# Two PSUM banks taken out of a shared tile after the attention stage, and a count loaded into registers earlier

## The chip, the cores and the metric

The kernel runs on one core of one Trainium2 chip. The metric is device time in microseconds (us) of that core; smaller is better. The engines are TensorE (PE, its weight loads apart as PEld), VectorE (DVE), ScalarE (ACT), GpSimd (POOL) and SyncE (SP, which issues most DMAs). An instruction that belongs to the engine's own sequencer (register loads, branches, semaphores, drains) carries a q behind the engine's name in the rows, as SPq.

## The reference, cut to what matters

Linear attention, then a mixture of eight experts of which each token uses two, then one large MLP. In code, with batch 4, 8 heads, 576 positions, head size 64 (so 2304 tokens of width 512):

```python
def phi(x):
    proj = einsum('bhsd,df->bhsf', x, w_phi)
    proj = proj - max(abs(proj), axis=-1)
    return concatenate([exp(proj), exp(-proj)])
q_p, k_p = phi(q), phi(k)
kv, z = einsum('bhsf,bhsd->bhfd', k_p, v), sum(k_p, axis=2)
x = (q_p @ kv) / (q_p . z + 1e-6)                  # -> [2304, 512]
logits = x @ w_gate + log1p(exp(x @ w_noise)) * noise
top2_w, top2 = softmax over the two largest of the 8 logits
x2 = sum over the two: top2_w * (relu(x @ w1[e]) @ w2[e])      # F = 1024
out = square(relu(x2 @ w_in)) @ w_out                          # 512 -> 2048 -> 512
```

## The kernel before

**Numbers.** All large products are float32 by three matmuls: each operand is split into a high and a low part (`hi_lo`, lines 94 to 96: ACT copies the high part, DVE subtracts), and high·high, low·high and high·low are added up in one PSUM bank. So every matmul of line 92 (`mm`) comes in threes, as `w31h,hh`, `w31l,hh`, `w31h,hl`.

**Order.** The program runs under a manual schedule: each engine executes its instructions in the order in which the code is written, and semaphores hold it where another engine's result is missing.

**Stages.** Attention, with the gating of the experts woven into it (some 0 to 263 us of the trace). At its end the tokens are ranked within their experts: `r_3b` (line 652, PE) counts, `r_4` (line 667, DVE) adds the counts to `runs`, the running number of tokens of each expert, `r_4b` makes `slots`, and `r_5` (line 737, POOL) scatters the rows of x to `xg_d` in device memory, at most CAP = 640 slots an expert. Then the experts, in ten parts `pt` (263 to 720 us; experts 0 and 7 are cut in two; 0 already starts inside the attention stage), and the last MLP in five blocks of up to 512 tokens (720 to 1124 us), called m.

**An expert part.** `x_t` (line 175) turns the gathered rows by PE transposes and splits them. Then for each of the eight column groups f: `e_1` (line 190) makes hidden activations in the banks M0 and M1, from which ACT makes `hh` (relu, line 213) and DVE `hl` (line 210); `e_2` (line 223) adds the second product, one group later, into five accumulators `YP[j]`, one for each 128 tokens, j = 0 to 4, which keep their bank over all f. After the last f, `e_y` (line 218) copies each accumulator out by ACT (`y`, line 220) and SP stores it. At a boundary between two experts the main loop (line 1104) issues the last group of the old expert for j = 0, 1, 2, then the first `e_1` of the new one, then j = 3, 4. The last MLP has the same form: `l_t` (line 981) turns the input x2 of a block, `l_1` (line 994) makes `h2h` and `h2l`, `l_2` (line 1013) adds into the same accumulators and copies them out as `o` (by ACT, line 1029, or DVE, line 1027).

**Banks.** PSUM has eight banks here: Tk, KV, M0, M1, N0, N1 as tiles of one bank, and one tile of two banks, `pair` (line 79), which holds the tags Tq and P. `bank` (line 81) hands out a tile or a half of `pair`. Dependences are kept by tile: a write to one half of `pair` waits for the last reader of either half. The attention stage needs the two banks as one tile for the q products and the norms; the accumulators use Tq as j = 0 and P as j = 2 (`ACC`, line 146).

**The end.** A token count above CAP would need a slow path. `runs` is reduced to its largest value and cast by DVE, then loaded into a register of all five engines (`values_load`, line 1162), and `tc.If(most > CAP)` (line 1165) branches around the slow path, which is not taken here. Both stand behind all other work. Line 1255 is the end of the program, where the engines are drained and meet.

Of the kernel before, what the change touches and what calls it, by code (L numbers as in the profile page):

```python
# [9 lines left out]
FT = mybir.dt.float32  # L10
FR = mybir.dt.float32r
BF = mybir.dt.bfloat16
I32 = mybir.dt.int32
U16 = mybir.dt.uint16
AF = mybir.ActivationFunctionType
OP = mybir.AluOpType
AX = mybir.AxisListType
# [15 lines left out]
def kernel(  # L33
# [15 lines left out]
    nc = tc.nc  # L49
# [5 lines left out]
    NT = B * S  # L55
# [4 lines left out]
    DC = DM // 128  # L60
# [4 lines left out]
    consts = ctx.enter_context(tc.tile_pool(name="consts", bufs=1))  # L65
# [3 lines left out]
    psum = ctx.enter_context(tc.tile_pool(name="psum", bufs=1, space=bass.MemoryType.PSUM))  # L69
# [6 lines left out]
    x_d = dram.tile([NT, DM], FT, name="x_d")  # L76
    g_d = dram.tile([NT, E], FT, name="g_d")

    pair = psum.tile([128, 2, 512], FT, tag="pair", name="pair")

    def bank(tag, shape):
        if tag not in PAIR:
            return psum.tile(shape, FT, tag=tag, name=tag)
        names = "abc"[:len(shape) - 1]
        n = 1
        for x in shape[1:]:
            n *= x
        return pair[:, PAIR.index(tag), :n].rearrange(
            f"p ({' '.join(names)}) -> p {' '.join(names)}", **dict(zip(names, shape[1:])))
# [4 lines left out]
    def hi_lo(hi, lo, src):  # L94
        nc.scalar.activation(hi, src, AF.Copy)  # L95
        nc.vector.tensor_sub(lo, src, hi.bitcast(FT))  # L96
# [6 lines left out]
    runs = consts.tile([128, E], FT)  # L103
# [39 lines left out]

    NJ = CAP // 128
    NF = F // 128
    ACC = ["Tq", "KV", "P", "N0", "N1"]
    parts = [(0, 0, JA), (0, JA, NJ)] + [(e, 0, NJ) for e in range(1, E - 1)] + [(E - 1, 0, JA), (E - 1, JA, NJ)]
    XG, XT, HT, YP, xp = {}, {}, {}, {}, [None]

# [25 lines left out]
    def x_t(pt, j):  # L175
        e = parts[pt][0]
        if pt not in XT:
            n = RA if pt == 0 else CAP
            XT[pt] = (x_tile(pt, [128, DC, n], FR, "xth", ("kp", 2)), x_tile(pt, [128, DC, n], FR, "xtl", ("kp", 2)))
            if pt == NP - 2:  # L180
                XT[pt + 1] = XT[pt]
        t = bank(["Tk", "M0", "M1"][j % 3], [128, DC, 128])
        for d in range(DC):
            nc.tensor.transpose(t[:, d], XG[pt, j][:, d * 128:d * 128 + 128], ident)  # L184
        c = x_cols(pt, j)
        hi_lo(XT[pt][0][:, :, c], XT[pt][1][:, :, c], t)
# [36 lines left out]
    def e_2(pt, f, js=None):  # L223
# [4 lines left out]
        for j in range(j0, j1) if js is None else js:  # L228
            if f == 0:
                YP[j] = bank(ACC[j], [128, DM])  # L230
            c = slice((j - j0) * 128, (j - j0) * 128 + 128)
# [5 lines left out]

    with ExitStack() as actx:
        xp[0] = ap_ = actx.enter_context(tc.tile_pool(name="attn", bufs=1))

        KT, KTT, VT, VTT, QT, QTT, NZ = {}, {}, {}, {}, {}, {}, {}

# [545 lines left out]
        for n in range(NU + 2):  # L788
            b, i = divmod(n, 9)
# [96 lines left out]
        e_2(0, NF - 1)  # L886


    wpb[0] = ctx.enter_context(tc.tile_pool(name="wpb", bufs=1))

    with ExitStack() as ectx:
        xp[0] = ep = ectx.enter_context(tc.tile_pool(name="experts", bufs=1))
# [88 lines left out]
        def l_t(m, i):  # L981
            ya, _ = YA.pop((m, i))
            if i == 0:
                X2[m] = [ep.tile([128, DC, 512], FR, name="x2", tag=x, bufs=1)
                         for x in (("xth", "xtl") if m % 2 == 0 else ("xg", "wd"))]
            t = bank("Tk" if m else ("Tk", "Tq", "KV", "M0")[i], [128, DC, 128])
            for d in range(DC):
                nc.tensor.transpose(t[:, d], ya[:, d * 128:d * 128 + 128], ident)  # L988
            c = slice(i * 128, i * 128 + 128)
            hi_lo(X2[m][0][:, :, c], X2[m][1][:, :, c], t)  # L990
# [22 lines left out]
        def l_2(u):  # L1013
# [4 lines left out]
            for j, tt in enumerate(blocks[m]):  # L1018
                if f == 0:
                    OP_[j] = bank(ACC[j], [128, DM])  # L1020
                c = slice(j * 128, j * 128 + 128)
# [114 lines left out]
        for i in range(R):  # L1136
            l_t(0, i)
        e_2(NP - 1, NF - 1)
        NU = len(blocks) * NF2
        for u in range(NU + 1):  # L1140
            m, f = divmod(u, NF2)
# [13 lines left out]
                if f in (5, 8, 11, 14) and (f - 2) // 3 - 1 < len(blocks[m + 1]):  # L1155
                    l_t(m + 1, (f - 2) // 3 - 1)

    cf = consts.tile([128, 1], FT)
    ci = consts.tile([128, 1], I32)
    nc.vector.tensor_reduce(cf, runs, axis=AX.X, op=OP.max)  # L1160
    nc.vector.tensor_copy(ci, cf)
    most = nc.values_load(ci[0:1, 0:1], min_val=0, max_val=2 * NT)


    with tc.If(most > CAP):
        with ExitStack() as sctx:
# [27 lines left out]
            with tc.For_i(0, NT, 128) as row:  # L1194
# [8 lines left out]
                for e in range(E):  # L1203
# [4 lines left out]
                    for f in range(F // 128):  # L1208
                        t = bank(f"M{f % 2}", [128, 128])
# [3 lines left out]
                    t = bank("P", [128, DM])  # L1213
# [5 lines left out]
                for n in range(F2 // GF):  # L1219
# [4 lines left out]
                    for f in range(GF // 128):  # L1224
                        t = bank(f"M{f % 2}", [128, 128])
# [15 lines left out]
def build(nc, inputs):  # L1241
    import numpy as _np
    import concourse.tile as _tile
    from concourse import mybir as _mybir
    arrays, args = {}, []
    for name in _INS:
        a = _np.ascontiguousarray(inputs[name])
        if a.dtype == _np.float64:
            a = a.view(_np.int64)
        arrays[f"in_{name}_dram"] = a  # L1250
        args.append(nc.dram_tensor(f"in_{name}_dram", a.shape, _mybir.dt.from_np(a.dtype), kind="ExternalInput").ap())
    for i, (shape, dtype) in enumerate(_OUTS):
        dt = _mybir.dt.from_np(_np.dtype(dtype))
        args.append(nc.dram_tensor(f"out_{i}_dram", shape, dt, kind="ExternalOutput").ap())
    with _tile.TileContext(nc) as tc:
        kernel(tc, *args)
    return arrays
# [11 lines left out]
```

## Time and profile before

| | |
|---|---|
| median of three runs | 1135.84 us (1135.78 to 1138.93) |
| profiled execution | 1136.58 us, its span 1134.8 us, mean granted TensorE clock 0.992 |
| busy, share of the span | PE 1095.5 us (97%), PEld 928.2 (82%), DVE 605.0 (53%), ACT 478.8 (42%), POOL 397.6 (35%) |
| chain of work that ended last | PE 73%, ACT 2%, DVE 1%, DMA 1% |

How to read it: the span runs from the first to the last instruction in the trace; the profiled execution's own time is 1.8 us longer than its span, and lies inside the range of the three runs. Busy shares are means over all stages. The chain is followed back from the last instruction, at each step to what released it.

### The profile page before, as it was taken

The page shows a single profiled execution, that of the slowest core. Times are in us where ns is not written, and L with a number is a line of the kernel's source. Part 1 is how long each engine was busy: PE and PEld are TensorE (multiplying, and loading weights), DVE is VectorE, ACT ScalarE, POOL GpSimd, SP SyncE. Part 2 cuts the span into 40 slices and gives each one's busy share as a digit, 9 for nine tenths or more (in the row PEclk, how much of TensorE's full clock was granted, in tenths as well). Part 3 has the DMA queues.
Part 4 walks back from the last instruction along what each step waited for, and adds up shares of the span by engine and source line. Part 5 has one row for each costly group of instructions (what it writes and reads, how often), then busy time and mean ns, then how long its engine had stood idle before and what let it go on. Part 6 is the DMA issues. An engine that isn't in the chain of part 4 may idle for free.

```text
span 1134.8 us, 17634 instructions
## 1 busy us (share of the span) xinstructions
PE 1095.5 (97%) x6652; PEld 928.2 (82%) x6652; DVE 605.0 (53%) x1197; ACT 478.8 (42%) x970; POOL 397.6 (35%) x374
## 2 busy tenths in 40 slices
PE   7999899999999999999999999999999999999996
PEld 5777677698898989898898989788898888888884
DVE  4566677771277767777777773342343333333222
ACT  4666566623434444444435353442232322232221
POOL 3333444654454645454545556461020100000000
PEclk9999999999999999999999999999999999999998
DMA  5777343236564546455554655332121101001001
GB/s 136 231 193 226 95 131 112 95 132 206 169 208 154 188 159 186 171 187 186 186 195 159 208 163 161 114 107 56 38 57 38 30 26 56 19 1 38 1 1 39
DMA packets 105468, 137.77 MB, mean 121 GB/s; under 512 B 17442, under 2 KB 59554, under 8 KB 105378
## 3 DMA queue, kind: packets, MB, share of 16 engines
q1 hardware_dynamic: 99618, 117.72, 32.9%
q0 software_dynamic: 5760, 18.88, 5.1%
q8 instruction: 54, 0.88, 0.3%
q14 instruction: 36, 0.29, 0.1%
HBM read 92.97 MB, written 43.59 MB: 120 GB/s over the span
## 4 chain that ended last, share of the span: by engine, by line
PE 73%; ACT 2%; DVE 1%; DMA 1%; issue 0%; SPq 0%; ACTq 0%
PE M L92 36%; PE pair L92 16%; PE N L92 12%; PE KV L92 8%; PE M L184 1%; PE Tk L184 1%; PE Tk L988 1%; DMA xg_d<-xt,slots 0%; DMA xs<-xg_d 0%; ACT y L220 0%; ACT r L1005 0%; DVE xtl L96 0%; ACT w30h L138 0%; ACT w10h L138 0%; ACT o L1029 0%
## 5 line engine op out<-in xcount | busy, mean ns | idle before, releaser
L1009 DVE TENSOR_TENSOR r<-M,r 128x512 f32<-128x512 f32 (+1 forms) x80 | 51.1, 638 | 247.3 <-ACT h2h L1008 247.3
L213 ACT ACTIVATE hh<-M 128x320 fp32r<-128x320 f32 (+2 forms) x128 | 50.9, 437 | 233.5 <-PE M L92 233.5
L1005 ACT ACTIVATE r<-M 128x512 f32<-128x512 f32 (+1 forms) x80 | 44.4, 555 | 248.0 <-PE M L92 248.0
L210 DVE SCALAR_TENSOR_TENSOR hl<-M,hh 128x320 fp32r<-128x320 f32 (+2 forms) x128 | 58.3, 487 | 123.7 <-ACT hh L213 123.4
L483 POOL PARTITION_ALL_REDUCE qmx<-ps x36 | 69.8, 1941 | 121.4 <-ACT ps L481 100.7
L970 POOL DMA_INDIRECT ya<-y_d,yrows x18 | 18.0, 998 | 188.8 <-PE Tk L988 113.3
L92 PE MATMUL N<-kvc,qp 128*128 128x81 f32 x512 | 65.7, 283 | 5.1 <-DVE ll L519 2.5
L92 PEld LDWEIGHTS N<-kvc,qp 128*128 128x128 f32 x512 | 61.4, 197 | 10.8 <-issue 5.5
L1010 DVE TENSOR_TENSOR h2l<-r,h2h 128x512 fp32r<-128x512 f32 (+1 forms) x80 | 57.7, 721 | 7.3 <-DVE r L1009 0.5
L96 DVE TENSOR_TENSOR ktl<-Tk,kth 128x512 fp32r<-128x512 f32 (+1 forms) x38 | 25.2, 664 | 53.5 <-ACT kth L95 53.5
L1008 ACT ACTIVATE h2h<-r 128x512 fp32r<-128x512 f32 (+1 forms) x80 | 47.1, 589 | 2.6
L92 PE MATMUL M<-x,w30h 128*128 128x512 f32 (+1 forms) x160 | 45.9, 371 | 0.0
L139 POOL TENSOR_TENSOR w20l<-wstage,w20h 128x512 fp32r<-128x512 f32 x20 | 28.1, 1406 | 50.4 <-ACT w20h L138 25.5
L92 PE MATMUL M<-x,w20h 128*128 128x512 f32 (+1 forms) x160 | 45.7, 370 | 0.0
L92 PE MATMUL M<-x,w10h 128*128 128x512 f32 (+1 forms) x160 | 45.7, 370 | 0.0
L92 PE MATMUL M<-x,w00h 128*128 128x512 f32 (+1 forms) x160 | 45.4, 368 | 0.0
L139 POOL TENSOR_TENSOR w30l<-wstage,w30h 128x512 fp32r<-128x512 f32 x20 | 27.4, 1370 | 51.1 <-ACT w30h L138 50.9
L742 POOL DMA_INDIRECT xg_d<-x,slots x32 | 32.9, 1027 | 15.6 <-DVE slots L703 9.4
L139 POOL TENSOR_TENSOR w10l<-wstage,w10h 128x512 fp32r<-128x512 f32 x16 | 22.2, 1390 | 40.2 <-ACT w10h L138 37.1
L940 POOL TENSOR_TENSOR wd<-wd 128x256 f32<-128x256 f32 x32 | 23.9, 746 | 35.3 <-DVE wd L936 34.6
L940 POOL TENSOR_TENSOR wx<-wx 128x256 f32<-128x256 f32 x32 | 23.7, 741 | 35.2 <-DVE wx L936 33.8
L92 PE MATMUL KV<-kp,vt 128*64 128x256 f32 x256 | 35.1, 395 | 0.3 <-ACT kvz L454 0.3
(385 smaller groups left out, 3402.9 us busy)
## 6 DMA issues: line engine op xcount, KB each, us to landing
wstage<-in_moe_w_dram SPq DMA_DIRECT2D x128, 256.0 KB, 3.7
xg_d<-zero SPq DMA_DIRECT2D x8, 1280.0 KB, 7.2
y_d<-y SPq DMA_DIRECT2D x40, 256.0 KB, 2.4
xg<-xg_d SPq DMA_DIRECT2D x7, 1280.0 KB, 6.8
wide<-in_moe_w_in_dram SPq DMA_DIRECT2D x32, 256.0 KB, 3.3
wide<-in_moe_w_out_dram SPq DMA_DIRECT2D x32, 256.0 KB, 2.9
kt<-in_k_dram SPq DMA_DIRECT2D x16, 256.0 KB, 4.2
vt<-in_v_dram SPq DMA_DIRECT2D x16, 256.0 KB, 3.3
```

The lines of the kernel that those rows point to most:

```text
L92: nc.tensor.matmul(o, l, r, start=start, stop=stop, skip_group_check=True)
L96: nc.vector.tensor_sub(lo, src, hi.bitcast(FT))
L139: (nc.gpsimd if n >= 2 else nc.vector).tensor_sub(lo[:, c], src, hi[:, c].bitcast(FT))
L210: nc.vector.scalar_tensor_tensor(hl[:, c0:c1], o, 0.0, hh[:, c0:c1].bitcast(FT), op0=OP.max, op1=OP.subtract)
L213: nc.scalar.activation(hh[:, c[1]:c[2]], c[0], AF.Relu)
L483: nc.gpsimd.partition_all_reduce(mx, ps, 128, bass.bass_isa.ReduceOp.absmax)
L742: st = nc.gpsimd.indirect_dma_start(out=xg_d, out_offset=bass.IndirectOffsetOnAxis(ap=slots[:, T0[g] + i, c:c + 1], axis=0), in_=src, in_o ...
L940: nc.gpsimd.tensor_mul(part, part, exp)
L1005: nc.scalar.activation(r[:, :n], t[:, :n], AF.Relu)
L1008: nc.scalar.activation(hh[:, :n], r[:, :n], AF.Square)
L1009: nc.vector.tensor_mul(r[:, :n], t[:, :n], r[:, :n])
L1010: nc.vector.tensor_sub(hl[:, :n], r[:, :n], hh[:, :n].bitcast(FT))
```

## The change

It has two parts. After the attention stage the tags Tq and P are two tiles of one bank each: `pair` lives in a pool of the attention stage alone (`ppsum`), and a new pool (`pbank`) serves both tags from there on. With it the accumulators are handed out in another order (`ACC`: j = 0 gets N0, j = 3 gets Tq), and the second tile of the first `l_t` goes to N0. And the reduction, the cast and the register load of the largest count are made once at the end of the attention stage and no longer ahead of the branch.

```diff
-    pair = psum.tile([128, 2, 512], FT, tag="pair", name="pair")
+    pair = None
+    pbank = psum
 
     def bank(tag, shape):
         if tag not in PAIR:
             return psum.tile(shape, FT, tag=tag, name=tag)
+        if pair is None:
+            return pbank.tile(shape, FT, tag=tag, name=tag)
...
-    ACC = ["Tq", "KV", "P", "N0", "N1"]
+    ACC = ["N0", "KV", "P", "Tq", "N1"]
...
         xp[0] = ap_ = actx.enter_context(tc.tile_pool(name="attn", bufs=1))
+        ppsum = actx.enter_context(tc.tile_pool(name="ppsum", bufs=1, space=bass.MemoryType.PSUM))
+        pair = ppsum.tile([128, 2, 512], FT, tag="pair", name="pair")
...
         e_2(0, NF - 1)
 
 
+    cf = consts.tile([128, 1], FT)
+    ci = consts.tile([128, 1], I32)
+    nc.vector.tensor_reduce(cf, runs, axis=AX.X, op=OP.max)
+    nc.vector.tensor_copy(ci, cf)
+    most = nc.values_load(ci[0:1, 0:1], min_val=0, max_val=2 * NT)
+
+
     wpb[0] = ctx.enter_context(tc.tile_pool(name="wpb", bufs=1))
+    pair = None
+    pbank = ctx.enter_context(tc.tile_pool(name="pbank", bufs=1, space=bass.MemoryType.PSUM))
...
-            t = bank("Tk" if m else ("Tk", "Tq", "KV", "M0")[i], [128, DC, 128])
+            t = bank("Tk" if m else ("Tk", "N0", "KV", "M0")[i], [128, DC, 128])
...
-    cf = consts.tile([128, 1], FT)
-    ci = consts.tile([128, 1], I32)
-    nc.vector.tensor_reduce(cf, runs, axis=AX.X, op=OP.max)
-    nc.vector.tensor_copy(ci, cf)
-    most = nc.values_load(ci[0:1, 0:1], min_val=0, max_val=2 * NT)
-
 
     with tc.If(most > CAP):
```

Where it shows in the order of the engines: PE at the boundary between two experts of five accumulators. `pair` is the accumulator of j = 0 and then of j = 2, `KV` that of j = 1, w31 the old expert's weights, `M` the first product of the new one. Before:

```order
L92 MATMUL pair<-w31h,hh 128x512 [waits Activation_49]
L92 MATMUL pair<-w31l,hh 128x512 [waits Pool_49]
L92 MATMUL pair<-w31h,hl 128x512
L92 MATMUL KV<-w31h,hh 128x512
L92 MATMUL KV<-w31l,hh 128x512
L92 MATMUL KV<-w31h,hl 128x512
L92 MATMUL pair<-w31h,hh 128x512 [waits Activation_49]
L92 MATMUL pair<-w31l,hh 128x512
L92 MATMUL pair<-w31h,hl 128x512
L92 MATMUL M_4414<-xth,w00h 128x320 [waits DVE_49]
L92 MATMUL M_4415<-xth,w00h 128x320
```

The same place on PE in the changed kernel:

```order
L95 MATMUL N_3925<-w31h,hh 128x512 [waits Activation_49]
L95 MATMUL N_3925<-w31l,hh 128x512 [waits Pool_49]
L95 MATMUL N_3925<-w31h,hl 128x512
L95 MATMUL KV<-w31h,hh 128x512
L95 MATMUL KV<-w31l,hh 128x512
L95 MATMUL KV<-w31h,hl 128x512
L95 MATMUL P<-w31h,hh 128x512 [waits Activation_49]
L95 MATMUL P<-w31l,hh 128x512
L95 MATMUL P<-w31h,hl 128x512
L95 MATMUL M_4443<-xth,w00h 128x320 [waits DVE_49]
L95 MATMUL M_4444<-xth,w00h 128x320 [waits Activation_49]
```

The instructions and their order are the same; j = 0 and j = 2 no longer write one tile. The wait of j = 2 on ACT was for the copy of j = 0 out of the other half; in its place stands a wait on ACT that counts only up to `hh` of that f, and the second `M` product has a wait for the new x's high part.

POOL at the end of the program: `ya` and `yb` are the gathers of the last block's input, `ci` is the largest count. Before:

```order
L970 DMA ya<-y_d,yrows 128x512 [waits DMASW4_49,DVE_49,PE_49]
L970 DMA yb<-y_d,yrows 128x512 [waits DMASW7_49]
L970 DMA ya<-y_d,yrows 128x512 [waits DMASW6_49,DVE_49,PE_49]
L970 DMA yb<-y_d,yrows 128x512 [waits DMASW1_49]
L1162 TENSOR_LOAD ci [waits DVE_49]
L1165 COMPARE_AND_BRANCH
```

The same place on POOL in the changed kernel:

```order
L984 DMA ya<-y_d,yrows 128x512 [waits DMASW4_49,DVE_49,PE_49]
L984 DMA yb<-y_d,yrows 128x512 [waits DMASW7_49]
L984 DMA ya<-y_d,yrows 128x512 [waits DMASW6_49,DVE_49,PE_49]
L984 DMA yb<-y_d,yrows 128x512 [waits DMASW1_49]
L1173 COMPARE_AND_BRANCH
```

The load, which waits for DVE's cast, has gone from between the last gather and the branch, and nothing there waits for DVE at the program's end any more.

PE near the end of the attention stage, where the last count of `r_3b` (rt_mask, onesb) stands ahead of `e_2` of expert 0 (w01). Before:

```order
L92 MATMUL pair<-rt_mask,onesb 128x8
L92 MATMUL pair<-w01h,hh_3219 128x512 [waits Activation_49]
L92 MATMUL pair<-w01l,hh_3219 128x512
L92 MATMUL pair<-w01h,hl_3220 128x512
L92 MATMUL KV<-w01h,hh_3219 128x512
```

The same place in the changed kernel:

```order
L95 MATMUL pair<-rt_mask,onesb 128x8
L95 MATMUL N_3195<-w01h,hh_3223 128x512 [waits Activation_49]
L95 MATMUL N_3195<-w01l,hh_3223 128x512
L95 MATMUL N_3195<-w01h,hl_3224 128x512
L95 MATMUL KV<-w01h,hh_3223 128x512
```

The accumulator of j = 0 has left the tile that holds the counts, which `r_4` on DVE reads next.

## Rows read from the trace of the kernel before

**Rows 1.** Waits of PE: who, released by whom, us in all, times, longest

```profile
PE pair L92 <- ACT y L220: 8.7, 6, 1.5
...
PE pair L92 <- ACT o L1029: 1.0, 2, 0.5
```

**Rows 2.** Timeline of PE at an expert boundary: start, us, what, [idle before, releaser]

```profile
359.55 0.39 PE L92 MATMUL KV<-w31l,hh 128*128 128x512 f32 x1
359.78 0.40 PE L92 MATMUL KV<-w31h,hl 128*128 128x512 f32 x1
361.63 0.50 PE L92 MATMUL pair<-w31h,hh 128*128 128x512 f32 x1 [1.46 <-ACT y L220]
361.96 0.39 PE L92 MATMUL pair<-w31l,hh 128*128 128x512 f32 x1
```

**Rows 3.** Timeline of ACT and DVE behind the same boundary

```profile
366.00 0.77 ACT L213 ACTIVATE hh<-M 128x320 fp32r<-128x320 f32 x2 [2.77 <-PE M L92]
366.47 0.89 DVE L210 SCALAR_TENSOR_TENSOR hl<-M,hh 128x320 fp32r<-128x320 f32 x2 [2.49 <-ACT hh L213]
```

**Rows 4.** Timeline of PE and DVE between the experts and the last MLP

```profile
718.38 0.50 PE L92 MATMUL pair<-w31h,hh 128*128 128x512 f32 x1 [0.70 <-DVE x L96]
...
718.84 0.68 DVE L96 TENSOR_TENSOR x<-M,x 128x512 fp32r<-128x512 f32 x1
...
720.56 0.62 PE L92 MATMUL M<-x,w00h 128*128 128x512 f32 x2
```

**Rows 5.** Timeline of PE at the end of the last MLP block

```profile
1121.83 0.40 PE L92 MATMUL KV<-w31h,h2l 128*128 128x512 f32 x1
1122.22 0.50 PE L92 MATMUL pair<-w31h,h2h 128*128 128x512 f32 x1
```

**Rows 6.** Timeline of PE, DVE and POOL at the last ranking of the tokens

```profile
248.68 0.27 PE L92 MATMUL pair<-rt_mask,onesb 128*128 128x16 bf16 x5
...
249.36 0.39 PE L92 MATMUL pair<-w01h,hl 128*128 128x512 f32 x1
...
249.79 0.18 DVE L671 TENSOR_TENSOR rt_rk<-pair,runs 128x24 f32<-128x24 f32 x1 [1.67 <-PE pair L92]
...
251.66 0.96 POOL L742 DMA_INDIRECT xg_d<-x,slots  x1 [2.36 <-DVE slots L703]
```

**Rows 7.** Chain that ended last, in order of time, at the attention stage's end

```profile
258.00 3.15 DMA xg_d<-xt,slots
```

**Rows 8.** Timeline of PE, ACT and POOL at the attention stage's end

```profile
262.72 0.40 PE L92 MATMUL KV<-w11h,hl 128*128 128x512 f32 x1
...
263.71 0.66 PE L184 MATMUL M<-ident,xs 128*128 128x128 f32 x4 [0.60 <-DMA xs<-xg_d]
...
264.45 0.60 ACT L95 ACTIVATE xth<-M 128x512 fp32r<-128x512 f32 x1 [3.72 <-PE M L184]
...
271.97 1.31 POOL L139 TENSOR_TENSOR w20l<-wstage,w20h 128x512 fp32r<-128x512 f32 x1 [13.01 <-DMA wstage<-in_moe_w_dram]
```

**Rows 9.** Line 1162, the register loads: ns min/median/max, first to last start us

```profile
L1162 PEldq TENSOR_LOAD <-ci x1: 533/533/533, 1124.9 to 1124.9; - x1
```

**Rows 10.** Line 1165, the branch: same columns

```profile
L1165 PEldq COMPARE_BRANCH  x1: 3922/3922/3922, 1125.5 to 1125.5; - x1
...
L1165 POOLq INC_SWDGE_SEM  x1: 1624/1624/1624, 1126.3 to 1126.3; - x1
```

**Rows 11.** Line 1255, the program's end: same columns

```profile
L1255 SPq EVENT_SEMAPHORE  x14: 17/28/1100, 1127.9 to 1134.7; - x14
...
L1255 POOLq DRAIN  x3: 51/107/5942, 1128.0 to 1134.5; - x3
L1255 SPq DRAIN  x3: 7/7/13, 1129.7 to 1134.2; - x3
```

**Rows 12.** Line 970, POOL's gathers: same columns

```profile
L970 POOL DMA_INDIRECT yb<-y_d,yrows x18: 945/949/1379, 693.3 to 978.6; - x18
```

**Rows 13.** Busy time by window: us, engines busy (x), PEclk, DMA share, GB/s

```profile
1034.00:1124.00 90.00, 89.41 (x392) 72.99 (x390) 24.11 (x36) 21.96 (x36) 0.00 (x0) 1.00 0.04 16
```

## The prediction

> **What bounds the kernel now.** I read the profile's page first: PE is busy for 97% of the span and makes up 73% of the chain that ended last, so the time can only move where PE waits, or in the stretch behind its last matmul. The view of PE's waits then tells what of this the change touches: in six places, 8.7 us in all, matmuls into `pair` wait for ACT's `y`, and in two more, 1.0 us, for `o` [rows 1]. With five accumulators at the six boundaries that are followed by another expert's last group (parts 2 to 7), the six are one each. The timeline of one shows the whole price [rows 2]: PE's matmuls of 512 columns start 0.23 us apart (359.55, 359.78), but between the last of j = 1 and the first of j = 2 lie 361.63 − 359.78 = 1.85 us, and the next start comes 0.33 instead of 0.23 after that. So a boundary costs 1.85 − 0.23 + 0.10 = 1.72 us where the row says 1.46 idle: **a pause costs its idle time and 0.26 us**, 0.16 for the overlap of two matmuls and 0.10 for the restart. Last I read the end of the program line by line [rows 9 to 11], and the attention stage's end, where PE is not the bound but the chain goes through scatters and loads [rows 6 to 8].
>
> **The change part by part.**
>
> *Boundaries between experts.* j = 2 waited for the copy of j = 0, since both were halves of one tile. Now they are two tiles, and of the wait only `hh` is left, made by ACT ahead of j = 0's own matmuls. Nothing is left to wait for: 8.7 + 6 × 0.26 = **10.3 us**. What follows comes 1.7 us earlier, so something else could be late next. Behind the boundary ACT was idle 2.77 us before its `hh`, waiting for PE, and DVE 2.49 us before its `hl`, waiting for `hh` [rows 3]; ACT's copies, made while PE paused, move against PE by at most those 1.72 us, which leaves about 1.05 and 0.77 us. So PE's next products find `hh` and `hl` ready. The cover is thin, though: were it gone, each boundary would give back what the copies push `hl` beyond 0.77. Lower bound: half of the term, 5.1, if `hl` is late everywhere; upper bound 10.3, since no other pause is there.
>
> *Into the last MLP.* The last group of expert 7 waits for DVE's split of the tile in Tq, 0.70 us [rows 4]; that tile is in N0 now and j = 0 there is N0 too, but for this two-tile part the accumulators are j = 3 and 4, Tq and N1, neither touched by the new `l_t`. By the rule of a pause this gives 0.70 + 0.26 = **0.96 us**. The floor below is DVE's last split, which ends at 718.84 + 0.68 = 719.52, while `l_1` starts to read at 720.56 and would come 0.96 earlier, at 719.60. It just holds; bounds 0.9 and 0.96.
>
> *Ends of the MLP blocks.* Four blocks have j = 2. Two pauses for `o` sum to 1.0 us [rows 1], so 1.0 + 2 × 0.26 = 1.5. At the other two PE shows no idle time, but a start 0.39 after the last (1121.83, 1122.22 [rows 5]), by the rows of the boundary 0.16 lost and 0.10 for the restart: 2 × 0.26 = 0.5. Together **2.0 us**; bounds 1.5 and 2.0.
>
> *Attention's end, the rank.* DVE's first step of `r_4` starts at 249.79, right behind the `pair` matmul of `e_2` that ends at 249.36 + 0.39 = 249.75; the counts it reads are ready at 248.68 + 0.27 = 248.95 [rows 6]. With j = 0 in N0 it starts 0.8 earlier. From it hang `slots` and then the last scatters, POOL being idle for 2.36 us before the first of them [rows 6]; the last scatter's DMA is on the chain [rows 7], and PE is idle before the transposes of the rows loaded behind it [rows 8]. So up to 0.8 us comes through. Against it stands the moved load. Each engine now does it in the attention's end: PE's took 0.53 us [rows 9] and stands between the last matmul at 262.72 and the transposes at 263.71, where PE sits idle for 0.60 us anyway [rows 8]; if the scatters are 0.8 earlier, the idle time is gone and the load lies bare: 0.53 − 0.60 + 0.8 is more than itself, so up to 0.53 of the 0.8 could be lost for the first transpose. But three loads of rows are waited for one by one, and the chain goes on through the last of them, which is behind the first. I take **0.6 us**, with bounds 0.3 and 0.8. On ACT the load is covered by 3.72 us of idle time and on POOL by 13.01 [rows 8]; DVE's stands ahead of the split that waits for that same ACT instruction; SP's stands behind its last load of rows and ahead of stores of `y`, which ACT has yet to make. If this cover were gone, each would cost its 0.5 us once.
>
> *The end of the program.* Before, all engines load the count at 1124.9 [rows 9] behind DVE's cast, and then branch. Two things take time then. PE's branch lasts 3.92 us, from 1125.5 to 1129.4 [rows 10], and SP waits 1.10 us, up to its drain at 1129.7 [rows 11]. POOL's branch is followed by a semaphore instruction of 1.62 us [rows 10] and a DRAIN from 1128.0 that lasts 5.94 us, to 1133.9; the span ends 0.9 later [rows 11]. After the change POOL's branch stands behind the last gather, issued at 978.6 [rows 12]; it and the DRAIN fall into the some 145 us up to 1124.9 in which POOL has no work. PE's branch follows its last matmul: six more start after 1122.22 [rows 5], so at about 1123.6, which ends at 1127.5, before SP gets there. SP still waits for the landing of the last stores, so the end is SP's: 1129.7 − 1.1 = 1128.6 instead of 1133.9, **5.3 us** earlier. Bounds: nothing, if POOL's DRAIN waits for something at the program's end and not for its own work; 5.9, POOL's DRAIN whole.
>
> The Trainium skill, "VectorE: DVE Perf Modes", section "The DRAIN you can't avoid", says that the DRAINs around a kernel take a constant 12 ns or so on all five engines. SP's (7 to 13 ns) agree, POOL's 5942 ns does not [rows 11]. By the page there is nothing to gain from POOL's and the tail would give SP's 1.1 us at most; the measured row decides.
>
> **Sum.** 10.3 + 0.96 + 2.0 + 0.6 + 5.3 = 19.2 us off the profiled execution's 1136.58 us: 1117.4. That execution is 0.74 above the median of the runs, 1135.84, so on the median I forecast 1135.84 − 19.2 = 1116.6, rounded to **1116.8**. The own range is 1114.5 to 1119.
>
> **The rivals.** *The tail does not give its 5.3 us.* Either POOL's DRAIN ends when the last DMA or the last engine ends, wherever it starts (for it: it carries no wait that would explain 5.94 us; against it: the other engines' drains, among them SP's, which stands behind the stores, take nanoseconds [rows 11]): 1136.58 − 13.9 = 1122.7 on the profiled, 1122 on the median. Or SP's branch stalls as PE's did, 3.9 us [rows 10], because it is now reached from another place in its instructions: SP then comes to its end at most 3.9 later, and the time is up to 1116.8 + 3.9 = 1120.7. The Trainium skill, "Runtime: NRT & Kernel Launch", section "Instruction fetch mechanics", has a rule for it: a taken branch whose target is outside the window of instructions already fetched stalls the engine for the fetch. PE's row agrees; no other engine's shows it. Chance of both: 0.14.
>
> *The boundary's pause comes back as another.* `hl` or `y` is late where the slack is 0.77 us, or the wait on ACT still counts past `y`. For it: the slack is thin at every boundary. Against it: `hh` is ahead of `y` in ACT's order, and DVE has 2.49 us free [rows 3]. Price: from half the term lost, 1116.7 + 5.1 = 1121.8, to all of it, 1127. Chance 0.09.
>
> *Slower: the pauses were what kept PE's clock up.* A PE without pauses might be granted less; the page shows clock 0.992 over the span. At half the clock each us of full-speed work takes two, so more than 19.2 + 3.4 = 22.6 us of it at the lower level would end above 1139.2. Against it: in the last 90 us of the MLP PE was busy for 89.41 at a granted clock of 1.00 [rows 13]. Chance 0.02.
>
> *The change does nothing,* because the pools' release makes all waits anew at the new tiles: the order shows that only the first use of the banks waits for the attention stage. Chance 0.01.
>
> **How the numbers follow.** The forecast has 0.74, the tail's rival 0.14, the boundary's 0.09, the clock 0.02, none 0.01. The forecast is 1116.8. Taking in the tail's rival (1120.7 and 1122) and half of the boundary's, and below the upper bounds of the tail and of the rank (0.6 and 0.2) with a run as low as the lowest before, the range is 1114.0 to 1122.5. A difference of 0.3%, 3.4 us, is about what a measurement of this kernel can tell from no change; all cases but the last two are far beyond it: faster 0.97, same 0.01, slower 0.02.
>
> **What would show it.** In the changed kernel's waits of PE the lines for `y` and for `o` are gone, and at each boundary the first matmul of j = 2 starts 0.23 us after j = 1's last; a new line of over 0.3 us at a boundary, for `hl` or `hh`, would show the second rival. The matmul ahead of `l_1` of block 0 has no wait for DVE. POOL's long DRAIN lies near 980 us and the span ends within 1.5 us of SP's last wait for stores; a DRAIN of some us at the end shows the tail's rival, a long branch on SP its other form. The load's rows stand at about 263 us, and `r_4`'s last start follows the counts by under 0.1 us. The prediction is wrong if the granted clock of a window in the experts falls, or if PE's bare load pushes the first `e_1` after the attention stage later than before.

## The result and the profile after

The changed kernel took 1120.47 us (median of 4 runs, 1115.74 to 1125.37), the kernel before 1135.81 us (4 runs, 1134.30 to 1138.93). The ratio is 0.986 with a 95% interval of 0.982 to 0.991: by it 15.7 us faster, between 10.3 and 21; the medians lie 15.3 apart. The profiled execution of the changed kernel took 1115.74 us (span 1114.0), 20.8 less than that of before. The forecast for the median was 1116.8.

Times of one kernel lie several us apart, so the trace is read stage by stage. The windows view of the changed kernel, cut where its attention stage ends and where its last matmuls start (us, engines busy with their instructions, granted clock, DMA share, GB/s):

```profile
0.00:120.00 120.00, 111.30 (x988) 82.04 (x988) 72.22 (x170) 75.11 (x143) 39.81 (x41) 1.00 0.67 190
120.00:264.00 144.00, 135.84 (x1279) 107.94 (x1278) 99.97 (x348) 78.23 (x157) 72.07 (x90) 1.00 0.36 121
264.00:1107.00 843.00, 841.47 (x4388) 734.36 (x4387) 432.16 (x679) 324.64 (x670) 284.25 (x244) 1.00 0.36 115
```

And that of the kernel before, with the same stages:

```profile
0.00:120.00 120.00, 111.05 (x996) 82.08 (x996) 73.08 (x175) 75.39 (x144) 40.67 (x41) 1.00 0.67 191
120.00:267.00 147.00, 139.79 (x1268) 111.99 (x1268) 99.64 (x342) 77.43 (x157) 72.24 (x90) 0.97 0.35 118
267.00:1124.00 857.00, 844.65 (x4388) 734.15 (x4388) 431.46 (x681) 325.94 (x672) 284.71 (x244) 1.00 0.35 113
```

The last row of each holds the experts and the last MLP. The windows are cut at whole us; between the starts of the same first and last matmul it is 13.1 us less. PE's idle time in the window falls from 12.4 to 1.5 us, at a clock of 1.00 in both. The row above it tells something else: some 3 us less in the attention stage, where the clock was 1.00 in one execution and 0.97 in the other. That part goes with the clock (below).

Waits of PE in that last window of the changed kernel (who, released by whom, us in all, times, longest):

```profile
PE M L95 <- DVE xtl L99: 2.2, 2, 1.5
PE N L95 <- DVE h2l L1024: 0.7, 1, 0.7
PE N L95 <- DVE hl L213: 0.2, 1, 0.2
```

These are all there are. The first stands in the kernel before too, and so does the second, there into `pair`. The waits for `y` and `o` of [rows 1] and the one for DVE's split of [rows 4] are gone. One is new, the last, 0.2 us for `hl`.

The timeline of PE at the boundary of [rows 2], start and us:

```profile
355.90 0.39 PE L95 MATMUL KV<-w31l,hh 128*128 128x512 f32 x1
356.13 0.40 PE L95 MATMUL KV<-w31h,hl 128*128 128x512 f32 x1
356.37 0.39 PE L95 MATMUL P<-w31h,hh 128*128 128x512 f32 x1
356.60 0.40 PE L95 MATMUL P<-w31l,hh 128*128 128x512 f32 x1
```

From the last matmul of j = 1 to the first of j = 2 it is now 0.24 us instead of 1.85, and the next follows after 0.23. ACT and DVE behind it, to compare with [rows 3]:

```profile
360.63 0.77 ACT L216 ACTIVATE hh<-M 128x320 fp32r<-128x320 f32 x2 [1.72 <-PE M L95]
...
361.10 0.89 DVE L213 SCALAR_TENSOR_TENSOR hl<-M,hh 128x320 fp32r<-128x320 f32 x2 [0.72 <-ACT hh L216]
```

DVE's idle time ahead of `hl` fell from 2.49 to 0.72 us. The slack of 0.77 that the prediction worked out was real, and enough. Where it was not is the two-tile part that follows the last boundary; the timeline of PE there:

```profile
662.18 0.40 PE L95 MATMUL N<-w31l,hh 128*128 128x512 f32 x1
662.73 0.50 PE L95 MATMUL N<-w31h,hl 128*128 128x512 f32 x1 [0.15 <-DVE hl L213]
```

0.55 between two starts instead of 0.23, and 0.33 to the next (663.06): the new wait costs 0.32 and 0.10, so 0.42 us by the starts. DVE and POOL just ahead of it (timeline):

```profile
660.58 1.47 POOL L142 TENSOR_TENSOR w00l<-wstage,w00h 128x512 fp32r<-128x512 f32 x1
...
660.94 1.40 DVE L959 SCALAR_TENSOR_TENSOR wd<-wd 128x256 f32<-128x256 f32 x1
662.26 0.74 DVE L213 SCALAR_TENSOR_TENSOR hl<-M,hh 128x256 fp32r<-128x256 f32 x2
```

And in the kernel before:

```profile
674.27 0.42 DVE L945 SCALAR_TENSOR_TENSOR wd<-wd 128x256 f32<-128x256 f32 x1
...
674.61 0.42 DVE L210 SCALAR_TENSOR_TENSOR hl<-M,hh 128x256 fp32r<-128x256 f32 x1
```

`wd` is a piece of the last MLP's weights that DVE prepares between its other work. Measured against PE's matmuls this step stands 0.7 us later than before, and it takes 1.40 us instead of 0.42, so the first `hl` (0.42 of the 0.74) ends right ahead of the matmul that reads it, where 1.4 us were to spare before. Of the 32 such steps of this line in the changed kernel's trace those with POOL at work beside them took 1.40 to 1.41 us, the others 0.42 to 0.43. In the kernel before POOL's split began at 674.33, just behind the step's start. On the way into the last MLP (timeline, for [rows 4]):

```profile
703.83 0.48 PE L95 MATMUL P<-w31h,hh 128*128 128x512 f32 x1
...
705.24 0.68 DVE L99 TENSOR_TENSOR x<-M,x 128x512 fp32r<-128x512 f32 x1
...
705.97 0.73 PE L95 MATMUL M<-x,w00h 128*128 128x512 f32 x2
```

P's first matmul has no wait. DVE's last split ends at 705.92 and `l_1` starts at 705.97: the floor named in the prediction is touched. Its first two matmuls take 0.73 us together instead of the 0.62 of [rows 4].

The attention stage's end, for [rows 6] and [rows 8] (timeline):

```profile
244.84 0.27 PE L95 MATMUL pair<-rt_mask,onesb 128*128 128x16 bf16 x5
...
245.15 0.18 DVE L676 TENSOR_TENSOR rt_rk<-pair,runs 128x24 f32<-128x24 f32 x1 [0.87 <-PE pair L95]
...
247.01 0.96 POOL L747 DMA_INDIRECT xg_d<-x,slots  x1 [1.59 <-DVE slots L708]
...
258.87 0.40 PE L95 MATMUL KV<-w11h,hl 128*128 128x512 f32 x1
...
259.97 0.66 PE L187 MATMUL M<-ident,xs 128*128 128x128 f32 x4 [0.70 <-DMA xs<-xg_d]
```

DVE starts `r_4` 0.04 us behind the counts, and POOL's wait for `slots` is 1.59 instead of 2.36: the scatters start 0.8 us earlier against PE's work in this execution. The chain that ended last, at the same place, gives it back, to compare with [rows 7]:

```profile
253.34 3.78 DMA xg_d<-xt,slots
...
258.07 3.58 DMA xs<-xg_d
```

The last scatter lands after 3.78 us instead of 3.15.

The register load (line 898), the branch (line 1173), the program's end (line 1263) and SP's last four stores (line 1046), ns min/median/max, first to last start, for [rows 9 to 11]:

```profile
L898 PEldq TENSOR_LOAD <-ci x1: 487/487/487, 257.6 to 257.6; - x1
...
L1173 SPq EVENT_SEMAPHORE  x8: 17/17/17, 1109.6 to 1112.3; - x8
...
L1173 PEldq COMPARE_BRANCH  x1: 3586/3586/3586, 1104.6 to 1104.6; - x1
...
L1263 SPq EVENT_SEMAPHORE  x14: 17/28/28, 1112.3 to 1113.9; - x14
...
L1263 POOLq DRAIN  x3: 51/107/5942, 968.2 to 1113.7; - x3
```

POOL's long DRAIN lies at 968.2, behind the last gather, and lasts the same 5942 ns: so it waits for nothing at the program's end. SP no longer waits for PE (longest semaphore 28 ns instead of 1100). The last matmul starts at 1106.75, so from there to the end of the span it is 7.2 us, against 11.3 before (1123.49 to 1134.75). But SP's eight waits for the stores end 5.5 us after that matmul's start (1112.3), where before they ended after 3.8 (1127.3). Why is seen in SP's store issues:

```profile
L1046 SPq DMA_DIRECT2D out_dram<-o x4: 332/522/805, 1105.8 to 1107.9; - x4
```

In the kernel before all four are 332 or 333 ns.

### The profile page after: what moved, and what is told of

It is laid out like the page before. It is cut to its first block, busy times and chain, and to the rows that moved or that the text cites. A ratio compares the mean times of both kernels' runs of the same rounds, so it can differ in the third digit from the quotient of the medians.

```text
span 1114.0 us, 17634 instructions
## 1 busy us (share of the span) xinstructions
PE 1088.8 (98%) x6652; PEld 924.3 (83%) x6652; DVE 605.0 (54%) x1197; ACT 478.1 (43%) x970; POOL 396.1 (36%) x374
## 4 chain that ended last, share of the span: by engine, by line
PE 91%; DVE 4%; ACT 2%; DMA 1%; issue 1%; POOL 1%; SPq 0%; POOLq 0%; ACTq 0%
PE M L95 40%; PE N L95 17%; PE KV L95 13%; PE Tq L95 8%; PE P L95 8%; PE pair L95 1%; PE M L187 1%; PE Tk L376 1%; PE Tk L386 1%; PE Tk L187 1%; PE Tk L1002 1%; DVE ktl L99 1%; DVE kd L415 0%; DVE kmx L412 0%; POOL xg_d L747 0%
```

## The experiments

For each run the document gives the time against the kernel before on the same chip and, from its trace, the stretch from the first product of expert part 1 to the end of the span, and the tail, from the start of the last matmul to the end. For the kernel before these are 867.3 and 11.3 us, for the changed one 850.2 and 7.2.

**load_only**: the kernel before, with only the load moved.

```diff
+    nc.vector.tensor_reduce(cf, runs, axis=AX.X, op=OP.max)
+    nc.vector.tensor_copy(ci, cf)
+    most = nc.values_load(ci[0:1, 0:1], min_val=0, max_val=2 * NT)
     wpb[0] = ctx.enter_context(tc.tile_pool(name="wpb", bufs=1))
...
-    nc.vector.tensor_reduce(cf, runs, axis=AX.X, op=OP.max)
-    nc.vector.tensor_copy(ci, cf)
-    most = nc.values_load(ci[0:1, 0:1], min_val=0, max_val=2 * NT)
     with tc.If(most > CAP):
```

> Only the count's reduction, cast and register load stand at the end of the attention stage; the shared tile and the accumulators are as before. Theory (the two parts of the change add up, and the tail's part is POOL's long DRAIN taken off the end): 4 to 5.3 us faster than before, the stretch from PE's last matmul to the end of the span about 7 us instead of 11.3, and PE's six waits for y unchanged. If the stores at the end land later because PE's branch now fetches its instructions beside them, the issues of the last stores show more than 0.33 us each here too. Rival (the tail's gain needs the banks' change as well, or POOL's DRAIN comes back at the end): within 1.3 us of before.

1144.67 us against 1147.55, ratio 0.997 [0.9955, 0.9986], 2.9 us less where 4 to 5.3 were expected. The tail is 7.15 us, so at the program's end the load alone brings 4.1 us. The stores and the end:

```profile
L1039 SPq DMA_DIRECT2D out_dram<-o x4: 332/332/939, 1134.1 to 1136.5; - x4
...
L1166 SPq EVENT_SEMAPHORE  x8: 17/17/17, 1139.3 to 1140.8; - x8
...
L1166 PEldq COMPARE_BRANCH  x1: 4271/4271/4271, 1134.1 to 1134.1; - x1
```

The late stores come with the moved load. From the first product to the end it is 864.8 us, 2.5 less than before and not 4.1, because PE ran at the low clock for some us right behind that first product.

**banks_only**: only the banks, the load at the program's end.

```diff
+        if pair is None:
+            return pbank.tile(shape, FT, tag=tag, name=tag)
-    ACC = ["Tq", "KV", "P", "N0", "N1"]
+    ACC = ["N0", "KV", "P", "Tq", "N1"]
```

(and the pools, `pair` and `l_t` as in the change)

> Only the banks: Tq and P two tiles after the attention stage, with the accumulators and l_t as in the change; the count is loaded at the program's end as before. Theory: six boundaries 10.3, the last MLP's ends 2.0 to 2.3 and the way into it 0.95 us, so 13.3 to 14.2 us faster than before where both run at the same granted clock; POOL's DRAIN of 5.94 us at the end as before, and issues of the last stores of 0.33 us. Rival (the load at the end of the attention stage is what gives part of it, or the pauses come back elsewhere): under 10 us faster.

1134.94 us, ratio 0.989 [0.987, 0.991], 12.6 us less. From the first product to the end 854.3 us, 13.0 less and just under the 13.3 to 14.2 expected; tail 11.4 with POOL's DRAIN in it. 13.0 and 4.1 make the 17.1 of the whole change, so its parts add up.

**order_only**: one shared tile throughout, only the accumulators' order and `l_t`'s bank changed.

```diff
-    ACC = ["Tq", "KV", "P", "N0", "N1"]
+    ACC = ["N0", "KV", "P", "Tq", "N1"]
-            t = bank("Tk" if m else ("Tk", "Tq", "KV", "M0")[i], [128, DC, 128])
+            t = bank("Tk" if m else ("Tk", "N0", "KV", "M0")[i], [128, DC, 128])
```

> The kernel before with one shared tile throughout and the load at the end; only the accumulators' order and l_t's second bank are those of the change, so the two halves of the shared tile are j = 2 and j = 3 and no longer j = 0 and j = 2. Theory (what cost time was that two halves stood one tile apart in one run of last groups): at the six boundaries the first product of the next expert stands between j = 2 and j = 3 and covers the copy, 10.3 us are gained as with two tiles; at the last group of expert 7 and at four block ends j = 3 follows j = 2 at once and waits for its copy, so there a pause of some 1.5 us and four of up to 0.7 stay or come. Together some 9 to 10 us faster than before. Rival (the shared tile itself costs at every boundary, whatever the order): PE waits for y at six places again, and the time is within 3 us of before.

1140.07 us, ratio 0.994 [0.992, 0.996], 7.5 us less; 859.1 from the first product to the end, 8.2 less, where 9 to 10 were expected. Its waits of PE for copies:

```profile
PE pair L92 <- ACT o L1029: 2.8, 4, 0.7
...
PE pair L92 <- ACT y L220: 1.0, 2, 0.7
```

At the six boundaries nothing is left of the pause: with P and Tq as j = 2 and j = 3 the next expert's first product stands between the two halves and covers the copy. What comes instead are pauses at all four block ends, 0.7 each where there were two of 0.5, and two short ones, behind the sixth boundary and at the last group of expert 7. So most of the banks' gain comes with the order alone; with that order the tile cut in two is worth some 5 us more. What the cut would bring in the old order, no run shows.

**after_again, before_again, after_third**: both kernels once more, unchanged, on a chip where the kernel before takes some 12 us longer than in the first runs.

> The changed kernel once more, unchanged, for the spread of its runs and for a second profile. Theory (the spread from 1115.7 to 1125.4 us is the granted clock: stretches of a few us at half clock, some 1.7 us each, more of them in one run than in another): each run's time falls with its clock, from about 1116 at 0.999 to about 1125 at 0.987, the stretches lie in the attention stage, and the pauses of the experts are gone in every profile. Rival (a wait that comes in some runs only): two runs of one clock lie more than 2 us apart.

> The kernel before once more, for a profile of it beside the changed kernel's on one chip. Theory (the change acts behind the attention stage alone, and what differs ahead of it is the granted clock of single stretches between 120 and 260 us): from the first product of part 1 to the end of the span 867.3 us as in the first profile, within 0.5 where the clock is 1.00 there; the start of that product anywhere from 264 to 282 us, in step with the clock. Rival (the two-bank tile's other place makes the attention stage slower): the start lies some 4 us before that of every kernel with the new banks.

> The changed kernel, for a third profile. Theory: 850.2 us from the first product of part 1 to the end of the span, as in its two others, so 17.1 less than before; the start of that product moves with the clock and not with the kernel. Rival (the two-bank tile's place): it starts some 4 us later than in the kernel before of the same chip at the same clock.

On that chip the kernel before took 1147.55 us (17 runs) and 1147.84 (16), the changed one 1133.58 and 1131.09: ratios 0.988 [0.985, 0.990] and 0.986 [0.983, 0.989]; before_again itself 1149.07 (12 runs), ratio 1.000 [0.998, 1.001]. From the first product to the end: 867.2 for before, 850.3 and 851.7 for the changed kernel, the last with 1.6 us lost to a stretch of low clock right behind the first product. So outside such stretches this part repeats, and the change takes 17.1 us from it in the first traces and 16.9 here. That first product starts at 280.4 us in before_again, at 281.4 and 276.9 in the two others, and at 267.4 and 263.8 in the first two traces. Most of what differs ahead of it is the clock, as in after_again:

```profile
0.00:120.00 120.00, 110.85 (x997) 82.11 (x998) 73.38 (x175) 75.70 (x145) 40.80 (x41) 1.00 0.68 192
120.00:281.00 161.00, 148.83 (x1268) 118.31 (x1268) 101.10 (x343) 76.91 (x157) 71.78 (x89) 0.92 0.33 107
281.00:1125.00 844.00, 841.78 (x4388) 734.58 (x4388) 431.82 (x681) 325.61 (x672) 284.51 (x244) 1.00 0.36 115
```

A clock of 0.92 over 161 us means that some 26 of them passed at half clock, which costs some 13 us (an estimate from this row). The product starts 17.6 us later than in the first trace of the changed kernel; where the other 4 to 5 come from, no run shows. The rival of a slower attention stage through the tile's place finds no support: the start of before_again lies between those of the changed kernel. What after_again's theory said of the spread fails in part: at a mean clock of 0.987 the changed kernel took 1125.37 us in the first runs and 1133.58 to 1134.95 here, so the mean clock alone does not give the time. It takes in the end too, where PE has no work and the clock is 0.50, and that end is longer in the kernel before; so equal means are not equal attention stages.

**late_pe and late_act_dve**: the changed kernel, with one cast on DVE behind its last copy and branches that wait for it.

```diff
+    cl = consts.tile([128, 1], I32)
+    nc.vector.tensor_copy(cl, cf)
+    nc.values_load(cl[0:1, 0:1], engines=(mybir.EngineType.PE,), ...)     # late_pe
+    nc.values_load(cl[0:1, 0:1], engines=(mybir.EngineType.Activation, mybir.EngineType.DVE), ...)     # late_act_dve
     with tc.If(most > CAP):
```

> The changed kernel with one small cast on DVE behind its last copy, for which PE's branch waits, so that PE branches some 1.4 us after its last matmul starts and not 2.15 us before. Theory A (the last stores are late because PE fetches its branch's target beside them): the last two store issues are 0.33 us each again, not 0.7 to 0.9, the stores land 1.2 us earlier, and the end waits for PE's branch: 6.3 to 6.6 us from the last matmul's start to the end instead of 7.2. Theory B (ACT's or DVE's branch beside the stores does it): the issues stay long, and the tail is 7.2 or longer. Theory C (any branch that is early, and by chance of the moment): one of the issues long, one short.

> The same with ACT's and DVE's branches held back and PE's early as in the changed kernel. Theory A (PE's branch is what delays the stores): the last store issues stay at 0.7 to 0.9 us and the tail at about 7.2 us. Theory B (ACT's or DVE's): issues of 0.33 us, stores that land at 3.5 us after the last matmul's start instead of 5.2, and a tail of about 5.7 us, which would be 1.5 us better than the changed kernel.

Neither A nor B alone: late_pe came out as B says, late_act_dve nearer to A, so either early branch is enough. late_pe: 1131.49 us, ratio 0.985 [0.982, 0.988], tail 7.8; its first three issues are short, its last takes 1.05 us, and SP's waits end 6.1 us after the last matmul's start. late_act_dve: 1130.99, 0.985 [0.983, 0.988], tail 7.55; the second issue takes 0.82 us, the last 0.40, and the stores land no earlier. (The value loaded is not used; only the wait stays, on the branch.)

**hold_three, hold_act_dve, late_three**: the same with four more copies on DVE, so that the branches come at 2.0 us instead of 1.35 after the last matmul's start; late_three holds all three engines by the one cast.

```diff
+    for _ in range(4):
+        nc.vector.tensor_copy(cl, cl)       # hold_three, hold_act_dve
+    nc.values_load(cl[0:1, 0:1], engines=(PE, Activation, DVE), ...)     # hold_three, late_three
```

> The changed kernel with a cast and four small copies on DVE behind its last copy, for which the branches of PE, ACT and DVE wait; POOL's stays early. All three then branch about 2.0 us after the start of PE's last matmul, as in the kernel before. Theory D (the stores are delayed by whichever engine branches, and so fetches instructions, while they are issued or landing): all four issues 0.33 us, the last store landed 3.5 us after the last matmul's start and not 5.1 to 5.7; PE's branch, 3.5 to 4.3 us, then sets the end, a tail of 6.6 to 7.3 us. Rival (something else of the early load, not the branches, delays the stores): long issues and a landing past 5 us as in the changed kernel.

> The same with only ACT and DVE held to about 2.0 us and PE branching early. Theory D: the store issued about 2 us after PE's branch is long (0.6 to 0.9 us), the last one short, the last store lands at 3.5 to 4.5 us, and the tail is 5.7 to 6.8 us, better than the changed kernel's 7.2. Rival (PE's early branch alone makes the landing late): landing past 5 us and a tail of 7.2 or more.

> The same with all three held by one cast only, to about 1.35 us, when the last store is being issued. Theory D: the first three issues 0.33 us, the last longer or its landing past 5 us. Rival (only a branch ahead of the issue counts): all issues 0.33 us and landing at 3.5 us, a tail of 6.0 to 6.6 us.

hold_three: 1122.33 us against 1135.89 on this chip, 0.987 [0.984, 0.990], tail 7.45. Its stores, branch and waits:

```profile
L1046 SPq DMA_DIRECT2D out_dram<-o x4: 332/332/333, 1113.2 to 1115.3; - x4
...
L1179 SPq EVENT_SEMAPHORE  x8: 17/17/17, 1116.3 to 1118.3; - x8
...
L1179 PEldq COMPARE_BRANCH  x1: 4122/4122/4122, 1116.3 to 1116.3; - x1
```

The last matmul starts at 1114.17, so SP's waits end after 4.1 us: the stores are quick again, and PE's branch sets the end. hold_act_dve: 1120.57, 0.987 [0.985, 0.988], tail 7.6:

```profile
L1046 SPq DMA_DIRECT2D out_dram<-o x4: 332/394/878, 1113.0 to 1115.2; - x4
...
L1179 SPq EVENT_SEMAPHORE  x8: 17/17/17, 1116.8 to 1119.9; - x8
...
L1179 PEldq COMPARE_BRANCH  x1: 3794/3794/3794, 1111.9 to 1111.9; - x1
```

With PE's alone of the three early the waits end 5.9 us after the last matmul's start (1114.02), so for this run the rival held and not theory D, by which the last store would have landed early: PE's early branch is enough, and so, by late_pe, are ACT's and DVE's. late_three, one run, 1122.61 us:

```profile
L1046 SPq DMA_DIRECT2D out_dram<-o x4: 332/332/332, 1112.7 to 1114.9; - x4
...
L1177 SPq EVENT_SEMAPHORE  x8: 17/17/17, 1115.9 to 1117.9; - x8
```

All issues are short, the waits end 4.2 us after the last matmul's start (1113.73), and the tail is 6.70. The three branches come while the last store is being issued, so here too the rival held: what counts is whether a branch is taken ahead of the issue of a store. The same kernel, timed:

> The kernel with PE's, ACT's and DVE's branches held by one cast once more, timed: it is the version with the shortest end so far. If its tail of 6.7 us is no accident, the last store's issue is 0.33 us, its landing under 4 us and the tail 6.5 to 6.9 us again, 0.5 us below the changed kernel's 7.2; from the first product of part 1 to the end 849.6 to 849.8 us. The time is then some 17.5 us below the kernel before's at the same granted clock, and within what the runs spread it is not told apart from the changed kernel (14 to 19 us faster than before).

1131.20 us against 1147.03, ratio 0.986 [0.983, 0.988], tail 6.75, and 849.7 us from the first product to the end. It is 0.5 us better than the changed kernel by the trace, and not told apart from it by its times.

## Why the prediction was right, and where its terms were off

The sign and the range held, and the mechanism is the one that was forecast: PE's pauses go, and POOL's DRAIN leaves the end. The median lies 3.7 us above the forecast. The range reached that far for rivals of the tail that did not come true (POOL's DRAIN at the end, a long branch on SP); that other shortfalls fell within it is in part luck. Term by term, by the starts of the same matmuls in both traces:

- *Boundaries*, 10.3 forecast. Each first matmul of j = 2 came 1.62 us nearer to j = 1's last, and the next 0.10 more: six times 1.72 give 10.3 us, and banks_only repeats it to 0.01 at each. The rival of another wait came true in small: 0.4 us for `hl`, in the two-tile part behind the sixth boundary. The prediction had read the slack in a part with five tiles and let it stand for all; it did not count DVE's work on `wd`, which in this part came to lie beside POOL's.
- *Into the last MLP*, 0.96 forecast, 0.94 at the first matmul, of which 0.86 is left once `l_1` runs. The prediction took the part ahead of it for one of two tiles; it has three, and P comes first. As `l_t` doesn't touch P either, the term stands.
- *Block ends*, 2.0 forecast, 2.3 measured: 0.4, 0.8, 0.8 and 0.3.
- *Rank and load at attention's end*, 0.6 forecast. The rank came 0.8 us earlier as worked out in the profiled execution (0.04 us behind the counts), but 0.5 to 0.8 us behind them in seven of the eleven traces with the new order, for which no run shows the reason. PE's load, costed at up to 0.5, cost nothing: at 257.6 it ran while queued matmuls still went on to 258.87. Nothing was won: from the last scatter's issue to the first product of part 1 it is 10.5 us instead of 9.4. The step that failed is that the scatters' head start goes through to the end of the chain. Their landing decides, and it varies: 3.2 to 3.3 us to SP's next load in the three traces of kernels with the late rank, 2.9 to 4.5 in those with the early one. Why, stays open.
- *End of the program*, 5.3 forecast, 3.9 to 4.1 measured, in load_only and in three traces of the changed kernel. The reasoning on POOL was right, to the nanosecond of its DRAIN. The term was mis-sized in SP's part: "SP still waits for the landing of the last stores" took the landing as fixed, but the branches of PE, ACT and DVE, now taken before or between the last stores, delay these: SP's waits end 1.7 us later against the last matmul. The prediction let PE's branch start behind its last matmul; it started 2.15 us before that one's start. The span ends 1.7 us behind SP's last wait, where 1.5 was named as the most.
- *Sum and range.* The terms make 1116.6; 1116.8 is no rounding of it, and the lower end of 1114.0 does not follow from the bounds named. Both change nothing here.

From the first product of part 1 to the last matmul these terms make 13.1 us (10.3, 0.9 and 2.3 less the 0.4), and the traces show 13.1; with the tail it is 17.2, against 18.6 forecast for the same terms. The rest of the 20.8 us of the first two profiles is the attention stage, 3.6 us, where the clock was 0.97 against 1.00: that those two profiles lie as far apart as forecast, and further, is luck.

The median came 15.3 us lower, less than 17.2. Taking 867.3 or 850.2 us and the 1.8 between span and time from the medians leaves 266.7 us for the attention stage of the kernel before and 268.5 for the changed one in the first runs, and 278.5 and 278.7 against 281.6 and 279.1 in the later ones. So in the timed runs that stage, with any stretch of low clock right behind it, came out some 0.4 to 3 us longer with the change. Of the ten traces of kernels with the moved load four have such a stretch at the first product or just behind it (after_third, load_only, late_pe, hold_act_dve), and lose 1.5 to 2.3 us by it; of the four with the load at the program's end none has. Whether the moved load has a part in that, or too few runs were looked at, isn't settled: the clock of the timed runs is a mean over all stages.

The rival of the clock has a grain of truth in another place than was thought: PE's clock fell in the attention stage, with and without the change. Behind it it stood at 1.00 with pauses and without, but for those stretches right at the first product. The prediction named a fall in the experts as a sign of being wrong; after_third has one there, of 3.4 us at 0.50, and it lies ahead of the first pause that was taken out.

## What to carry to other kernels

When two accumulators share a tile, look at which of them are written next to each other at the end of a sum: a copy out of one half stops the write of the other, and an order that puts other work between the halves gains as much at such a place as order and split together did here. A pause of a busy engine costs more than its row of idle time, here 0.26 us more, the overlap and the restart, and the cover for the next wait should be read in every part of the loop, with all that the engine does there and what runs beside it. Work that an engine can do early at a program's end, a branch or a drain, is worth moving off the end, but check what it runs beside: here early branches delayed the last stores, and the move brought 4.1 of the 5.3 us forecast. Holding the branches back gave no more than 0.5 us on top, as PE's own branch, 4.2 us long, then sets the end.

## What the runs showed of the hardware that was not expected

**PE's sequencer runs ahead of its matmuls.** PE's branch started at 1104.60, before the last ten matmuls had started (the last at 1106.75), and its register load ran beside matmuls still being worked off. So PE's register load of 0.49 us between matmuls showed no cost.

**Branches disturb stores.** With the branches of PE, ACT and DVE behind the start of the last store's issue the four issues took 0.33 us each and SP's waits for the stores ended 3.8 to 4.2 us after the last matmul's start (before, hold_three, late_three). With PE's, or ACT's and DVE's, ahead of it one or two issues took 0.55 to 1.05 us and the waits ended after 5.5 to 6.1 (the changed kernel, load_only, late_pe, late_act_dve, hold_act_dve). PE's branch itself took 3.5 to 4.3 us in every trace. The Trainium skill, "Runtime: NRT & Kernel Launch", section "Instruction fetch mechanics", says that a taken branch out of the fetched window makes a DMA fetch of its target necessary; that such a fetch meets the stores on the way is argued from it. No run here shows a fetch, or separates a branch from the end instructions that its engine runs behind it.

**PE's clock fell, while PE had work, only in the attention stage's second half and shortly behind it**, between 120 and 290 us, in stretches of 3.4 to 10 us at a granted clock of 0.50, and not in the same places in each execution. One in the kernel before, from 140.3 to 143.7 us, begins shortly behind a wait of PE for DVE:

```profile
139.63 3.10 PE L92 MATMUL N<-kvc,qp 128*128 128x81 f32 x16 [0.74 <-DVE ll L519]
```

In the changed kernel the same sixteen matmuls behind the same wait took 1.98 us, at a clock of 1.00, so the wait alone does not bring the fall:

```profile
138.90 1.98 PE L95 MATMUL N<-kvc,qp 128*128 128x81 f32 x16 [0.73 <-DVE ll L524]
```
